# An attention and feed-forward kernel whose planner gets new tables of order rules, with more spare matmuls and more score banks on the full array

## The chip, the core and the metric

The kernel runs on one core of a Trainium2 chip. A core has five engines that run their own instruction streams side by side and meet only at semaphores: TensorE (PE; PEld is its weight load), VectorE (DVE), ScalarE (ACT), GpSimd (POOL) and SyncE (SP), which here issues all DMA transfers. Matmul results land in PSUM, which the program uses as eight banks of 512 float32 columns on 128 partitions. The metric is the time of one execution on the device in microseconds; the median of three runs is 1193.63 us (1188.23 to 1194.63).

## What is computed

```python
xn = _layernorm(x)                                    # x: 1 x 2048 x 512, bfloat16
q, k, v = split_heads(xn @ wqkv)                      # H = 32 heads of 16
scores = einsum("bhqd,bhkd->bhqk", q, k) * 16 ** -0.5
o = einsum("bhqk,bhkd->bhqd", softmax(scores), v)
attn = merge_heads(o) @ wo
ffn = (silu(xn @ w1) * (xn @ w3)) @ w2                # F = 1792
return x + attn + ffn
```

The work that sets the time is the 32 x 2048 x 2048 scores: each is computed twice, goes once through a maximum and once through an exponential.

## The kernel before

**Two passes over the scores.** The 2048 queries are cut into four quarters of 512 and the heads into eight groups of four; a *unit* is 256 queries of one group (128 in the first two units and in the last four groups), 73 units in all. In the first pass (`p1`, line 1319) a matmul puts 128 queries on the partitions of a bank and 512 keys on its columns. One head has 16 numbers, padded to 32 rows, so such a matmul uses a 32-row strip of the array, a quarter of it, and four heads' matmuls can run side by side in four strips. DVE then takes the maximum over two banks in one instruction (line 1364, `part<-ps`, 128 x 1024 numbers), here called a *reduce*. There are 998 of them and 13 of another form (`SPLIT`, lines 1357, 1420, 1423 and 1432), for which ACT prepares half of the work. From the maxima of a unit POOL makes the negated maximum, which goes as two more rows into the padded queries (`Z`, `Zs`, `QT`), by DMA, and in the first and last units by PE (`ident,Z`) and ACT or DVE.

In the second pass (`p2`, line 1601) a matmul puts 128 keys on the partitions and 256 queries on the columns, so that the scores come out transposed and less their maximum; two such matmuls fill a bank, and ACT turns it into exponentials in the tile `PT` (line 1626, or 1657 where two neighbouring banks go through one instruction, a *pair*). The units in pieces of 128 queries take four matmuls for a bank. Instead of a strip, a bank of the second pass can be computed on the full array (*wide*): DMA copies the queries of one head into a matrix `BD` (128 rows, zero outside that head's 32), and a matmul with all 128 rows of keys gives the same scores (`ps<-BD,KT`; line 721, or line 725 where it stands as four column strips among value products). The value products (`ps<-PT,Vaug`, line 725) are four matmuls side by side, one for each head, with 17 columns each: 16 of the value and one of ones, which gives the sum. ACT copies the result to `U`, DMA and POOL make the reciprocal (`Lc`, `Rc`, `R`) and POOL normalises it into `wk_on` or `on_b`; in the last units DVE does this alone.

**The rest** fills PE between scores: the projections (`xnT,w...`), the gate and up products with ACT and POOL making `hT` from them, and the output tiles (`OUT`, `w,hT` 14 matmuls, `wo` and `wol`, with x added by `xr,ident`). The last quarter's output tiles come in two parts, `OUTA` (19 matmuls of 512 columns, parked in `t1`, `a32`, `th` and `zg`) and `OUTB` (2 matmuls, added to the parked part by DVE, line 1147). When a planner's estimate of PE's load is low, a *spare group* is put into a free bank: the identity times `xnT` (`ps<-xnT,ident`), whose result nobody reads. A `p1` matmul may also be issued two or three times over for the same reason.

**What sets the order.** Nothing is looped on the chip: a planner in Python (`_Prog` and the closing loop of `_build`) writes all five streams out. It keeps an estimate of when each engine and each bank is free, asks `pick_dve`, `pick_act`, `pick_pe`, `pick_pool` and `pick_sp` for their earliest next step, and emits the earliest. `pick_pe` (line 2017) chooses among the next `p1` pair, the next second-pass bank, the next group of a tile, a spare group (`fill_cand`) and a wide bank, by limits in `K`. `heat` (line 1961) is its estimate of PE's load over the last 3.413 us; `HEAT_FILL` is the load under which a spare group is put in, `HEAT_WIDE` that under which a bank is taken wide, `HEAT_P1` that under which `p1` is repeated; `A_LEAD` and `ROW_LEAD` say how far ahead of DVE and ACT their matmuls are issued; `PAIR_WAIT`, `PAIR_DEPTH` and `P2_NEAR` bear on pairs. The limits are not the same throughout:

```python
        if p1_n[0] + p2_n[0] >= seg[0] * SEG:
            rule = TUNE[seg[0]] if seg[0] < len(TUNE) else 0
            ...
            for k_, v_ in SETS[rule].items():
                setattr(K, k_, v_)
```

Each time 12 more steps of the two passes have been planned (`SEG`; both passes together have 3072), the defaults `RULES` are set again and the entry of `SETS` that `TUNE` names for this stretch is laid over them.

## Time and profile before

| | us |
|---|---|
| median of three runs | 1193.63 |
| lowest and highest | 1188.23, 1194.63 |
| the profiled execution's own time | 1195.37 |
| its span, first to last instruction | 1193.6 |
| busy: PE, DVE, ACT, POOL | 1120.2, 1167.8, 1167.2, 453.2 |
| mean granted TensorE clock | 0.986 |

The profiled execution is 1.74 us over the median of the runs. A share of busy time counts an instruction from its start to its end, and instructions of one engine overlap at their ends, so an engine that is called busy throughout can still be slower than its shortest pitch; the pitch is read from runs of equal instructions. In rows of groups the columns are: line, engine, operation, tiles, shapes and count; then busy time and mean duration in ns; then idle time of the engine just before them, and what ended most of it. In rows of a timeline the first number is the start and the second the length until the last of the counted instructions ends. The granted clock is 1.00 at full speed.

### The profile page before, as it was taken

How to read it: one execution, taken by the hardware profiler on the slowest of the kernel's cores; microseconds unless marked ns; L12 is line 12 of the kernel's file. 1: busy time of each engine (PE TensorE's matmuls, PEld its weight loads, DVE VectorE, ACT ScalarE, POOL GpSimd, SP SyncE). 2: the span in 40 equal slices, each digit the busy share in tenths (PEclk: the TensorE clock that was granted, in tenths of full speed). 3: DMA queues.
4: the chain of work that ended last, by engine and by line, in shares of the span. 5: the costliest groups of instructions: out<-in, count | busy, mean ns of one | idle time of the engine just before them, and what ended most of it. 6: DMA issues, size and time to landing. Idle time of an engine off the chain costs nothing.

```text
span 1193.6 us, 35219 instructions
## 1 busy us (share of the span) xinstructions
PE 1120.2 (94%) x14470; PEld 517.1 (43%) x14609; DVE 1167.8 (98%) x1090; ACT 1167.2 (98%) x2202; POOL 453.2 (38%) x888
## 2 busy tenths in 40 slices
PE   8999999999999999999999999999999999998998
PEld 4433444443444433344444443433334443455664
DVE  8999999999999999999999999999999999999995
ACT  8899999999999999999999999999999999998998
POOL 7145544244422355324432226533442214541220
PEclk9999999999999999999999999999899999997999
DMA  8232232111111121111111122111110112001000
GB/s 247 76 74 75 70 84 61 38 37 42 33 42 36 35 63 42 34 40 33 41 31 28 34 54 56 42 39 41 30 30 24 35 37 62 23 22 21 19 16 24
DMA packets 141636, 55.88 MB, mean 47 GB/s; under 512 B 103968, under 2 KB 141476, under 8 KB 141476
## 3 DMA queue, kind: packets, MB, share of 16 engines
q1 hardware_dynamic: 141476, 53.63, 17.5%
q8 instruction: 115, 1.88, 0.7%
q14 instruction: 45, 0.37, 0.1%
HBM read 38.93 MB, written 6.74 MB: 38 GB/s over the span
## 4 chain that ended last, share of the span: by engine, by line
ACT 49%; DVE 27%; PE 20%; DMA 2%; issue 2%; POOL 1%; SPq 0%; DVEq 0%; POOLq 0%
ACT PT L1626 35%; DVE part L1364 26%; PE ps L721 7%; ACT PT L1657 7%; PE ps L1601 4%; PE ps L725 4%; PE ps L1319 3%; ACT zg L1037 1%; ACT th L1031 1%; ACT ub L1041 1%; ACT U L1721 1%; ACT RB L1432 1%; ACT kq L909 1%; DMA R<-rd 1%; POOL Rc L1746 1%
## 5 line engine op out<-in xcount | busy, mean ns | idle before, releaser
L1364 DVE TENSOR_REDUCE part<-ps 128x2 f32<-128x1024 f32 x998 | 1134.7, 1212 | 9.6 <-PE ps L1601 5.4
L1626 ACT ACTIVATE PT<-ps 128x512 bf16<-128x512 f32 x1640 | 874.6, 688 | 10.1 <-PE ps L1601 6.3
L1601 PE MATMUL ps<-QT,KT 32*128 32x256 bf16 (+1 forms) x3634 | 475.2, 261 | 15.1 <-ACT PT L1626 3.0
L1319 PE MATMUL ps<-KT,QT 32*128 32x512 bf16 x2158 | 439.8, 387 | 12.7 <-DVE part L1364 5.9
L1601 PEld LDWEIGHTS ps<-QT,KT 32*128 32x128 bf16 x3634 | 169.9, 93 | 179.9 <-ACT PT L1626 72.3
L1657 ACT ACTIVATE PT<-ps 128x1024 bf16<-128x1024 f32 x204 | 222.3, 1116 | 1.5 <-PE ps L1601 1.3
L725 PE MATMUL ps<-PT,Vaug 128*17 128x256 bf16 (+1 forms) x4672 | 193.7, 263 | 3.4 <-DVE part L1364 0.8
L1319 PEld LDWEIGHTS ps<-KT,QT 32*128 32x128 bf16 x2158 | 109.5, 91 | 154.2 <-DVE part L1364 71.2
L721 PE MATMUL ps<-xnT,w 128*128 128x512 bf16 (+3 forms) x583 | 148.0, 320 | 12.3 <-ACT U L1721 4.4
L1746 POOL TENSOR_TENSOR Rc<-Lc,mone 128x8 f32<-128x8 f32 (+1 forms) x69 | 105.0, 1521 | 119.4 <-DMA Lc<-U 118.8
L725 PEld LDWEIGHTS ps<-PT,Vaug 128*17 128x17 bf16 x4672 | 90.7, 90 | 80.7 <-issue 54.1
L721 PE MATMUL ps<-BD,KT 128*128 128x256 bf16 (+1 forms) x676 | 117.5, 268 | 3.7 <-ACT PT L1657 1.8
L1493 POOL TENSOR_TENSOR mx<-part 128x16 f32<-128x16 f32 (+1 forms) x60 | 14.2, 237 | 196.8 <-DVE part L1364 196.8
L721 PE MATMUL ps<-w,hT 128*128 128x128 bf16 (+3 forms) x349 | 81.6, 295 | 3.3 <-ACT U L1721 2.3
L721 PEld LDWEIGHTS ps<-xnT,w 128*128 128x128 bf16 x628 | 47.3, 97 | 83.3 <-issue 41.9
L721 PE MATMUL ps<-xnT,ident 128*128 128x512 bf16 (+3 forms) x244 | 66.5, 329 | 11.0 <-ACT PT L1657 3.8
L1008 POOL TENSOR_SCALAR t<-th 128x512 f32<-128x512 bf16 x56 | 34.9, 623 | 100.5 <-ACT th L1031 98.8
L1012 POOL TENSOR_TENSOR hT<-a,t 128x512 bf16<-128x512 f32 x56 | 71.1, 1269 | 2.7
L721 PEld LDWEIGHTS ps<-BD,KT 128*128 128x128 bf16 x676 | 53.4, 98 | 35.8 <-ACT PT L1626 8.0
L1782 POOL TENSOR_TENSOR on_b<-U,R 128x256 bf16<-128x256 f32 (+1 forms) x33 | 23.4, 710 | 117.4 <-DMA R<-rd 117.1
L1782 POOL TENSOR_TENSOR wk_on<-U,R 128x256 bf16<-128x256 f32 (+1 forms) x36 | 22.9, 637 | 110.2 <-DMA R<-rd 110.2
L1010 POOL TENSOR_TENSOR a<-zg,ub 128x512 f32<-128x512 bf16 x56 | 64.7, 1155 | 0.0
(114 smaller groups left out, 727.4 us busy)
## 6 DMA issues: line engine op xcount, KB each, us to landing
w<-in_B_w_dram SPq DMA_DIRECT2D x112, 128.0 KB
R<-rd SPq DMA_DIRECT2D x55, 128.0 KB
QT<-qd SPq DMA_DIRECT2D x31, 128.0 KB
KT<-kd SPq DMA_DIRECT2D x28, 128.0 KB
BD<-QT SPq DMA_DIRECT2D x220, 10.5 KB
xr<-in_A_x_dram SPq DMA_DIRECT2D x16, 128.0 KB
out_dram<-osb SPq DMA_DIRECT2D x16, 128.0 KB
qd<-kq SPq DMA_DIRECT2D x15, 128.0 KB
```

Of the source, the lines that this page charges most:

```text
L721: return e.matmul(bank(bk)[:, c0 + a:c0 + b], make_lhsT(0, 128), rhs_ap(0)[:, a:b], start=start, stop=stop, **kw)
L725: ins = e.matmul(bank(bk)[32 * i:32 * i + m, c0 + a:c0 + b], make_lhsT(i), rhs if (a, b) == (0, ncols) else rhs[:, a:b], start=start, stop ...
L1008: q.append(_Item(lambda e: e.tensor_scalar(t1[:, :], th[:, ss, :], 1.0, 1.0, ALU.mult, ALU.add), [("th", ss)], [("t1",)], 0.62, 0.72))
L1010: q.append(_Item(lambda e: e.tensor_tensor(a32[:, :], zg[:, ss, :], ub[:, ss, :], ALU.mult), [("zg", ss), ("ub", ss)], [("a32",)], 1.1, 1.25))
L1012: q.append(_Item(lambda e: e.tensor_tensor(hT[:, hslot(idx), :], a32[:, :], t1[:, :], ALU.mult), [("a32",), ("t1",)], [("hT", hslot(idx))] ...
L1319: ins = e.matmul(bank(held[i]), QT[32 * j:32 * j + 32, qs, q * 128:(q + 1) * 128], KT[32 * j:32 * j + 32, g, c_ * 512:(c_ + 1) * 512], sta ...
L1364: redq.append(_Item(lambda e: e.tensor_reduce(dst, banks, AX.X, ALU.max), writes, [("part", par, i_) for i_ in ix[:m]], _c_dve(512 * m), c ...
L1601: ins = e.matmul(bank(b)[:, i * nq:(i + 1) * nq], KT[32 * j:32 * j + 32, g, (k0 + i) * 128:(k0 + i + 1) * 128], QT[32 * j:32 * j + 32, qs, ...
L1626: expq.append(_Item(lambda e: e.activation(PT[:, sl, :], bank(b), ACTF.Exp, scale=SCALE), [("ps", b)], [("PT", sl)], _c_act(512), cb=cb, e ...
L1657: return _Item(lambda e: e.activation(PT[:, s0:s1 + 1:s1 - s0, :], two_banks(b0, b1), ACTF.Exp, scale=SCALE), [("ps", b0), ("ps", b1)], [( ...
L1746: poolq["nrm"].append(_Item(lambda e: e.tensor_tensor(Rc[:, pp, 0:nl], Lc[:, pp, 0:nl], mone[:, 0:nl], ALU.pow), [("Lc", pp), ("mone",)], ...
L1782: poolq["nrm"].append(_Item(lambda e: e.tensor_tensor(onorm[ob][:, oslot(ob, g), q0:q0 + nq], U[:, us, 0:nq], R[:, pp, 0:nq], ALU.mult), [ ...
```

## The change

Two tables of `_build` are replaced, and nothing else. `SETS` grows from 82 to 134 entries and `TUNE` from 254 to 256; before, 38 stretches used the plain defaults, and now 22. `HEAT_FILL` is set in 62 stretches instead of 34.

```diff
     SETS = (
         dict(),
         dict(A_LEAD=0.88, RELAX=0.1),
-        dict(A_LEAD=0.69),
+        dict(PAIR_WAIT=0.15, RELAX=0.05),
+        dict(P2_FRAG=0.0, URG_WAIT=0.05, A_LEAD=0.82, PAIR_WAIT=0.15),
...
     TUNE = (
-        1, 2, 3, 4, 5, 6, 7, 8, 0, 9, 10, 11, 0, 12, 13, 14, 15, 16, 17, 18, 19, 20, 21, 22,
+        1, 2, 3, 4, 5, 6, 7, 8, 9, 10, 11, 0, 12, 13, 0, 14, 15, 16, 17, 18, 19, 20, 21, 22,
...
```

The lines behind the tables stand 52 further down in the new kernel (1319 becomes 1371, 1601 becomes 1653, 721 becomes 773, 725 becomes 777, 1626 becomes 1678, 1657 becomes 1709). In the two orders as a whole, PE's instructions grow from 14611 to 15173. Of the 2048 banks of the second pass, 468 are wide before and 573 now. Spare groups are 311 before and 415 now (345 of them whole matmuls, 70 in four strips). ACT's pairs are 204 before and 160 now. DVE's, POOL's and SP's instructions are the same in kind and number, but for one parked part of an output tile that DVE takes from ACT.

Two places are shown, both on PE. The first is the slots of reduces 941 to 943 (of 1011), in the units of 128 queries near the end. `KT,QT` is the first pass, `QT,KT` the second in strips, `BD,KT` the second on the full array. Before:

```order
L1319 MATMUL ps<-KT,QT 128x512 x2
L1601 MATMUL ps<-QT,KT 128x128 x4
L721 MATMUL ps<-xnT,ident 128x512
L721 MATMUL ps<-xnT,ident 128x384
L1319 MATMUL ps<-KT,QT 128x512 x2
L1601 MATMUL ps<-QT,KT 128x128 x16
L721 MATMUL ps<-xnT,ident 128x512
L1319 MATMUL ps<-KT,QT 128x512 x2
L1601 MATMUL ps<-QT,KT 128x128 x8
```

The same three slots now:

```order
L1371 MATMUL ps<-KT,QT 128x512 x2
L773 MATMUL ps<-BD,KT 128x128 x8
L777 MATMUL ps<-PT,Vaug 17x128 x12
L1371 MATMUL ps<-KT,QT 128x512 x2
L773 MATMUL ps<-BD,KT 128x128 x8
L777 MATMUL ps<-PT,Vaug 17x128 x4
L1371 MATMUL ps<-KT,QT 128x512 x2
L1653 MATMUL ps<-QT,KT 128x128 x4
L773 MATMUL ps<-BD,KT 128x128 x4
L1653 MATMUL ps<-QT,KT 128x128 x4
L773 MATMUL ps<-xnT,ident 128x384
```

Seven banks in strips and three spare groups have become five wide banks, two banks in strips, value products and one spare group.

The second place is the end of PE's stream, from the last but one row of second-pass banks; `w,hT`, `wo` and `wol` belong to output tiles. Before:

```order
L1601 MATMUL ps<-QT,KT 128x128 x12
L721 MATMUL ps<-wol,wk_on 128x512 x3
L725 MATMUL ps<-PT,Vaug 17x128 x4
L1601 MATMUL ps<-QT,KT 128x128 x12
L725 MATMUL ps<-PT,Vaug 17x128 x16
L1601 MATMUL ps<-QT,KT 128x128 x8
L725 MATMUL ps<-PT,Vaug 17x128 x92
L721 MATMUL ps<-wol,wk_on 128x512 x2
L725 MATMUL ps<-PT,Vaug 17x128 x16
L721 MATMUL ps<-wol,wk_on 128x512 x2
```

Now:

```order
L773 MATMUL ps<-w,hT 128x512
L1653 MATMUL ps<-QT,KT 128x128 x12
L773 MATMUL ps<-w,hT 128x512 x3
L1653 MATMUL ps<-QT,KT 128x128 x12
L773 MATMUL ps<-w,hT 128x512 x10
L773 MATMUL ps<-wo,wk_on 128x512 x2
L773 MATMUL ps<-wol,wk_on 128x512 x4
L777 MATMUL ps<-PT,Vaug 17x128 x64
L773 MATMUL ps<-wol,wk_on 128x512 x2
```

The last `OUTA` tile, done in before ahead of these rows, now stands with 14 of its 19 matmuls behind the last score bank, and the last unit's 64 value products stand behind it. Behind the matmuls of the last reduce, 34 second-pass banks follow in before and 37 now; behind the row of the last unit's negated maximum (`ident,Z`), 26 and 30.

193 lines of the change are left out of this document (122 added, 71 removed), and 20 rows, old and new, of the table TUNE.

## The prediction

> **What bounds the kernel now.** I read the page first (busy shares, slices, the chain, the costliest groups), then the stretches of half clock, then the end. Lines of the page:
>
> ```profile
> PE 1120.2 (94%) x14470; PEld 517.1 (43%) x14609; DVE 1167.8 (98%) x1090; ACT 1167.2 (98%) x2202; POOL 453.2 (38%) x888
> ...
> PEclk9999999999999999999999999999899999997999
> ...
> L1364 DVE TENSOR_REDUCE part<-ps 128x2 f32<-128x1024 f32 x998 | 1134.7, 1212 | 9.6 <-PE ps L1601 5.4
> L1626 ACT ACTIVATE PT<-ps 128x512 bf16<-128x512 f32 x1640 | 874.6, 688 | 10.1 <-PE ps L1601 6.3
> L1657 ACT ACTIVATE PT<-ps 128x1024 bf16<-128x1024 f32 x204 | 222.3, 1116 | 1.5 <-PE ps L1601 1.3
> ```
>
> DVE (VectorE) holds 998 reduces, and a run of seven of them shows their pitch: (8.00 - 1.21) / 6 = 1.13 us.
>
> ```profile
> 1164.91 8.00 DVE L1364 TENSOR_REDUCE part<-ps 128x2 f32<-128x1024 f32 x7
> ```
>
> So the question is where DVE does not run at that pitch. Busy time by stretch answers it; columns are length, then busy time of PE, weight load, DVE, ACT and POOL, and the granted clock:
>
> ```profile
> 331.53:338.40 6.87, 6.87 (x109) 3.02 (x107) 6.18 (x6) 6.20 (x14) 0.72 (x1) 0.75 0.09 26
> 614.84:621.70 6.86, 5.98 (x62) 2.30 (x64) 6.14 (x6) 6.28 (x11) 5.06 (x6) 0.75 0.09 29
> 846.94:857.20 10.26, 9.79 (x61) 2.83 (x63) 8.05 (x9) 7.83 (x15) 1.60 (x5) 0.67 0.21 50
> 1089.29:1109.80 20.51, 19.08 (x352) 11.83 (x344) 16.48 (x16) 16.65 (x31) 4.70 (x9) 0.58 0.10 21
> sum 44.50, PE 41.72 PEld 19.99 DVE 36.84 ACT 36.96 POOL 12.09; mean PE 10.43 PEld 5.00 DVE 9.21 ACT 9.24 POOL 3.02
> ```
>
> ```profile
> 0.00:13.96 13.96, 10.99 (x93) 7.87 (x93) 10.48 (x29) 9.66 (x23) 6.55 (x25) 1.00 0.89 287
> 13.96:331.53 317.57, 299.62 (x3496) 129.56 (x3536) 316.57 (x283) 310.53 (x576) 140.43 (x251) 1.00 0.26 67
> 338.40:614.84 276.44, 261.05 (x3088) 115.31 (x3117) 276.42 (x250) 276.30 (x533) 108.49 (x212) 1.00 0.16 40
> 621.70:846.94 225.24, 213.28 (x2559) 94.42 (x2576) 224.82 (x204) 223.91 (x416) 90.65 (x172) 1.00 0.16 41
> 857.20:1089.29 232.09, 217.44 (x3084) 102.82 (x3105) 232.00 (x211) 231.94 (x444) 81.56 (x181) 1.00 0.13 32
> 1109.80:1172.90 63.10, 60.16 (x1257) 38.23 (x1258) 62.47 (x61) 62.51 (x132) 13.39 (x29) 1.00 0.08 17
> 1172.90:1193.60 20.70, 15.92 (x355) 8.94 (x357) 8.21 (x26) 15.38 (x21) 0.00 (x0) 0.95 0.08 27
> ```
>
> The span is 13.96 us before the first reduce, 1158.94 us of reduces, and 20.70 us behind the last. Between, DVE stands 44.50 - 36.84 = 7.66 us in the four stretches that begin at half clock, and only 1.00 + 0.02 + 0.42 + 0.09 + 0.63 = 2.16 us in all the rest. A stop also loses the 1.21 - 1.13 = 0.08 us by which reduces overlap; some 20 reduces follow a stop there, so the half clock costs about 7.66 + 1.6 = 9.3 us.
>
> The half clock itself lasts 3.41, 3.41, 6.83 and 17.07 us, multiples of 3.41:
>
> ```profile
> 331.53:334.94 3.41, 3.41 (x35) 1.23 (x33) 3.25 (x3) 3.10 (x7) 0.72 (x1) 0.50 0.03 8
> 614.84:618.25 3.41, 3.08 (x18) 1.12 (x16) 2.69 (x3) 3.05 (x5) 1.69 (x2) 0.50 0.14 45
> 846.94:853.77 6.83, 6.36 (x32) 1.61 (x33) 4.87 (x6) 4.76 (x9) 1.60 (x5) 0.50 0.29 70
> 1085.88:1089.29 3.41, 2.55 (x55) 1.50 (x50) 3.41 (x4) 3.41 (x6) 0.28 (x2) 1.00 0.10 24
> 1089.29:1106.36 17.07, 15.80 (x291) 9.91 (x286) 13.17 (x13) 13.24 (x25) 3.31 (x6) 0.50 0.12 23
> ```
>
> What stands ahead of the longest, in the 3.41 us from 1085.88, by shape, and a row that gives the time of a column:
>
> ```profile
> L1601 PE MATMUL ps<-QT,KT 32*128 32x128 bf16 x32 | 1.8, 217 | 0.2 <-ACT PT L1657 0.2
> L1319 PE MATMUL ps<-KT,QT 32*128 32x512 bf16 x6 | 1.2, 384 | 0.6 <-ACT PT L1626 0.4 <-DVE part L1364 0.2
> L725 PE MATMUL ps<-PT,Vaug 128*17 128x128 bf16 x16 | 0.5, 240 | 0.1
> L721 PE MATMUL ps<-xnT,ident 128*128 128x512 bf16 x1 | 0.4, 389 | 0.0
> ```
>
> ```profile
> 1178.39 1.04 PE L721 MATMUL ps<-w,hT 128*128 128x512 bf16 x4
> ```
>
> I call load the columns streamed, each counted with the quarter of the array that it fills (score matmuls and value products a quarter, others whole). Here (32 x 128 + 6 x 512 + 16 x 128) / 4 + 512 = 2816 columns. By the x4 row a column takes (1.04 - 0.39) / 3 / 512 = 0.42 ns, so 3.41 us hold 8060 columns: load 0.35. Counted in this way over the order of before, in windows of three reduces (3 x 1.13 us), the mean is 0.58, and 40 of 997 windows lie under 0.40. All four stops follow at once on one of these 40 (those from reduce 277, 527, 730 and 941). Of the 40, which stand in 29 places, four were followed by half clock.
>
> **The change, part by part.** Only the two tables differ, so no kind of instruction is added; the counts are from the two orders.
>
> Head, reduces, GpSimd, DMA: 0. DVE's rows are the same up to the last reduce (998, with the same 13 split rows), PE's the same for the first 57 rows; POOL and SP hold 892 and 1044 instructions in both. Steps move against them: the copies that fill BD stand earlier or later on SP's queue. Their cover is the unit's lead before its banks; uncovered, it would show as reduces or exponentials that wait for a bank, which is part of the 2.16 us. I leave that at 2.16, between 0 and 5.
>
> Thin load: windows under 0.40 go from 40 to 15, the mean from 0.58 to 0.60. At one stop for each ten, 1.5 stops are left. A short stop costs 6.87 - 6.18 us and two lost overlaps of 0.08, 0.85 us, and the mean of the four is 9.3 / 4 = 2.3. I take the short one, as the stretch around reduce 941, whose long half clock fed itself on 128-column work, rises to 0.56. So 1.3 us remain of 9.3 (bounds 0 and 3.5): -8.0 us.
> The Trainium skill (TensorE: Matmul & The Clock Gate, Terms) prices a throttled time at its length times the missing share, an estimate of 30.72 x 0.5 = 15.4 us here instead of 9.3; with the same 1.5 stops, the sum would fall to 1195.4 - 15.4 + 2.6 + 3.9 = 1186.5 us. The trace does not bear it out: DVE stands 7.66 us in and behind these stretches, since work stands ahead of it in the banks.
>
> More load to carry: 105 score banks move from quarter matmuls (1580 to 1475) to full-array matmuls over BD (468 to 573), and spare groups stream 140,500 columns for 118,700. A bank is two matmuls of 256 columns: on the full array 2 x 0.11 us of PE to itself, as quarters four banks in 0.22, 0.05 each; 105 x 0.16 = 17 us, and 21,900 x 0.42 ns = 9 us. These 26 us lie in PE's 1193.6 - 1120.2 = 73.4 us of idle time, and each reduce's two matmuls still stand ahead of them in its slot. I take 0 (bounds 0 and 26).
>
> Fewer pairs: 160 exponentials of two banks for 204. ACT's rows near the end show both prices:
>
> ```profile
> 1174.55 0.64 ACT L1626 ACTIVATE PT<-ps 128x512 bf16<-128x512 f32 x1
> 1175.03 1.08 ACT L1657 ACTIVATE PT<-ps 128x1024 bf16<-128x1024 f32 x1
> 1175.94 0.67 ACT L1626 ACTIVATE PT<-ps 128x512 bf16<-128x512 f32 x1
> ...
> 1187.42 0.87 ACT L1626 ACTIVATE PT<-ps 128x512 bf16<-128x512 f32 x1
> ```
>
> A bank alone takes 0.48 us to the next start and a pair 0.91, so 44 x 0.05 = 2.2 us more on ACT. What hides it is ACT's lead in the middle, where DVE stops only for 2.16 us; without that cover it adds up to 2.2.
>
> The end is the loss. Rows of PE in before:
>
> ```profile
> 1185.72 0.69 PE L1601 MATMUL ps<-QT,KT 32*128 32x128 bf16 x8
> 1186.34 1.46 PE L725 MATMUL ps<-PT,Vaug 128*17 128x128 bf16 x92
> ...
> 1188.33 0.40 PE L725 MATMUL ps<-PT,Vaug 128*17 128x128 bf16 x16
> ```
>
> ACT runs without a gap to 1188.29, three banks in 0.48 + 0.91 = 1.39 us. Behind the negated maximum of the last unit (ident,Z) before has 26 banks to go, after 30: 4 x 0.46 = +1.8 us; behind the last reduce's matmuls it is 34 and 37, +1.4. I take 1.6. Then PE's last score bank ends at 1186.41, 1.9 us before ACT does; the 92 value products run in that time, and the last 16 follow the last exponential. In the new order 16 matmuls of 512 columns (14 of the last quarter's sum, two of another) stand there first, 16 x 0.217 = 3.5 us, and then all 64 value products, 64 / 92 x 1.46 = 1.0 us: they end 4.7 us after the last score bank, where those of before end at 1188.73, 2.3 us after it. +2.4 us, less a little since three banks, not two, are issued last: 2.3. So +3.9 (bounds: +0.8 if ACT was less behind and PE's rest ran in its waits, +5).
>
> Sum, against the profiled execution's own 1195.37 us: -8.0 + 0 + 0 + 3.9 = 1191.3 us. That execution stood 1.74 us over the median of the three shown, 1193.63; their spread (1188.23 to 1194.63) is what a different number of stops would make.
>
> **The rivals.**
> The end is hidden (0.24): ACT arrives with fewer banks behind it and PE's late matmuls fit in its waits. For it: PE is busy 15.92 of the last 20.70 us. Against: PE works in order, and the 16 stand ahead. Time 1187.4 with 1.3 us of stops, 1186.1 with none: faster.
> A stop costs half its length (0.03): the four of before then cost 30.72 / 2 = 15.4 us and 1.5 of them 2.6, which gives 1186.5; DVE's 7.66 us speak against it.
> The stops stay (0.11): thin load isn't what sets them, or new ones grow where the new order is thin (reduces 139, 170, 184). Then 1195.4 + 3.9 = 1199.3, or slower with one long stop more. Speaking for it: 36 of 40 thin windows went unpunished.
> By the Trainium skill (TensorE: Matmul & The Clock Gate, What's actually happening) the clock falls after an idle window of some 3.4 us, and PE wasn't idle in any: by that rule this rival would be the case. The trace speaks against it: 2.55 us of 3.41 busy, then half clock.
> PE becomes the bound (0.10, slower): the 26 us of added matmul time push reduces' matmuls back. It decides from 8.3 us of the 26 on the path: 1191.3 + 8.3 = 1199.6; at half of them, 1204. Against it: 2.16 us of DVE idle at full clock.
>
> **How the numbers follow.** My forecast has 0.52, and its own range is 1188 to 1195. What a measurement can tell here is about 0.5% of 1193.63, 6.0 us: faster is under 1187.7, slower over 1199.6. The hidden end and the half price are faster, 0.27, with 0.02 of mine at its edge; of the stops that stay half is slower, with PE as the bound 0.15; the same has 0.56. The range, 1185 to 1199, takes in the hidden end and half of the stops that stay, and leaves out PE as the bound and the worst stops.
>
> **What would show it.** Granted clock over 0.99 with at most two short stops (a mean of 0.986 again means the stops stayed). DVE idle between first and last reduce under 5 us, and the last reduce ending near 1165. Behind it 24 to 25 us, with ACT's last exponential some 17 us after the last reduce, and the value products behind the 16 long matmuls. I am wrong if DVE waits for score banks at full clock, or if the end is as long as before.

## The result, and the profile after

Over 20 executions of each, the changed kernel takes 1196.97 us (1192.32 to 1204.50) and the kernel before 1192.44 us (1188.17 to 1201.79): a ratio of 1.0040, 95% interval 1.0021 to 1.0059. The change makes the kernel slower by 0.4%; two more comparisons of the two kernels, in the table below, give 1.0012 and 1.0036, with intervals that reach down to 0.9987 and 1.0000. The prediction of 1191.3 us had the sign wrong; its range of 1185 to 1199 us holds the time.

The profiled execution of the changed kernel is a low one of its 20: 1193.87 us, with a span of 1192.1 us. The page, where L1416 is the reduce, L1678 the single exponential and L1709 the pair:

```profile
PE 1123.6 (94%) x15037; PEld 529.2 (44%) x15171; DVE 1166.7 (98%) x1091; ACT 1166.2 (98%) x2245; POOL 452.0 (38%) x888
...
PEclk9999999999999999999999999999999999999999
...
L1416 DVE TENSOR_REDUCE part<-ps 128x2 f32<-128x1024 f32 x998 | 1133.2, 1216 | 6.9 <-PE ps L1653 3.5
L1678 ACT ACTIVATE PT<-ps 128x512 bf16<-128x512 f32 x1728 | 918.8, 715 | 6.5 <-PE ps L1653 2.4
L1709 ACT ACTIVATE PT<-ps 128x1024 bf16<-128x1024 f32 x160 | 177.0, 1123 | 0.3 <-PE ps L1653 0.2
```

Busy time by stretch, cut at the first reduce, at the one stretch of half clock and at the last reduce:

```profile
0.00:14.25 14.25, 10.84 (x93) 7.77 (x93) 10.47 (x29) 9.67 (x23) 6.99 (x25) 1.00 0.91 285
14.25:1095.69 1081.44, 1025.24 (x13132) 467.69 (x13250) 1077.20 (x969) 1069.37 (x2057) 428.77 (x831) 1.00 0.18 46
1095.69:1099.11 3.42, 3.08 (x29) 1.66 (x30) 1.50 (x2) 2.17 (x5) 0.00 (x0) 0.50 0.05 7
1099.11:1168.36 69.25, 65.91 (x1418) 42.30 (x1427) 68.57 (x67) 68.54 (x141) 15.76 (x32) 1.00 0.09 18
1168.36:1192.10 23.74, 18.52 (x369) 9.79 (x371) 8.93 (x26) 16.45 (x24) 0.46 (x1) 0.98 0.07 24
```

Three things are read from these. Of the 30.72 us of half clock between the reduces, 3.42 us are left. The end takes 23.74 us instead of 20.70. And DVE, which stood 2.16 us at full clock before, now stands 1081.44 - 1077.20 = 4.24 us ahead of the half clock and 69.25 - 68.57 = 0.68 us behind it; with 3.42 - 1.50 = 1.92 us at half clock it is idle for 6.84 us. Counted by starts of neighbouring reduces against their pitch of 1.13 us, the changed kernel loses 7.9 us between first and last reduce, and 5.6 of them at four places: 1.13 us at 79 and 83, 1.62 at 122, 2.06 at 1094 and 0.76 at 1142 us. (By the same count the profile of before loses 11.8 us, most of it in and just behind its half clock. The count leaves out a wait that begins behind another instruction of DVE, here 0.87 us at 1083 us, where PE waits 1.06 us for a copy into `BD`.) What PE waits for there, in the chain of waits (total, times, longest):

```profile
PE ps L773 <- POOL Z L1522: 2.7, 2, 2.0
PE ps L777 <- DMA BD<-QT: 2.6, 2, 1.5
...
PE ps L1653 <- DMA QT<-Zs: 1.1, 1, 1.1
```

The longest, row by row:

```profile
1093.74 0.45 POOL L1834 TENSOR_TENSOR wk_on<-U,R 128x128 bf16<-128x128 f32 x1 [6.01 <-DMA R<-rd]
1094.15 1.01 POOL L1798 TENSOR_TENSOR Rc<-Lc,mone 128x4 f32<-128x4 f32 x1
1095.14 0.21 POOL L1520 TENSOR_SCALAR Z<-negm 128x4 bf16<-128x4 f32 x1
...
1095.70 0.29 PE L773 MATMUL ps<-ident,Z 128*128 128x128 bf16 x1 [1.96 <-POOL Z L1522]
...
1097.10 1.22 DVE L1416 TENSOR_REDUCE part<-ps 128x2 f32<-128x1024 f32 x1 [1.97 <-PE ps L1653]
```

POOL works in order. The negated maximum is there at 1092.9 us (DVE's row 1092.70, 0.17 long), but `Z` stands behind a product that waits for the DMA of `R`. PE stands 1.96 us, DVE as long, and 0.01 us before PE starts again the clock falls to half; of the 3.41 us ahead of that, PE was busy for 1.36.

**The measure used below.** Single executions differ by some 10 us, and most of that follows the mean granted clock: from it, (1 - clock) x 2 x time is the time at half clock, and over the 29 to 35 executions of the kernel before in each of the five groups of runs, the time rises by 0.34, 0.35, 0.35, 0.35 and 0.34 us for each us at half clock, which accounts for 86 to 89% of its variance. (A group was run on one chip, the kernel before beside the others; the groups are those of the five sections below.) So each kernel gets two numbers: its median time at half clock, and its *clear time*, the mean of time less 0.34 us per us at half clock. The clear time has a standard error of 0.3 to 0.7 us. In the five groups the kernel before has clear times of 1185.7, 1185.4, 1185.7, 1185.7 and 1186.1 us, at 26 to 34 us of half clock, so kernels of different groups are compared by it. The slope is that of the kernel before; the 44 executions of the changed kernel give 0.39, with a standard error of 0.04. By that slope the gap of 7.3 us between the two kernels would be 6.6, and the 4.1 us that the mended queue brings below would be 3.7.

| kernel | median us | ratio to before, 95% | half clock us | clear us |
|---|---|---|---|---|
| before (five groups) | 1193.86 to 1196.24 | 1 | 26.3 to 33.5 | 1185.7 |
| changed, first 20 | 1196.97 | 1.0040 (1.0021 to 1.0059) | 13.2 | 1193.0 |
| again_before | 1191.45 | 0.9964 (0.9934 to 0.9993) | 17.9 | 1185.2 |
| again_after | 1199.14 | 1.0012 (0.9987 to 1.0037) | 18.0 | 1193.7 |
| after_other_end | 1203.19 | 1.0039 (1.0012 to 1.0065) | 27.7 | 1192.6 |
| after_no_spare_load | 1249.22 | 1.0406 (1.0360 to 1.0451) | 229.4 | |
| changed_third | 1199.89 | 1.0036 (1.0000 to 1.0072) | 20.4 | 1192.9 |
| no_three_waits | 1205.03 | 1.0069 (1.0033 to 1.0104) | 25.3 | 1196.3 |
| value_products_first | 1202.96 | 1.0042 (1.0007 to 1.0077) | 21.7 | 1195.6 |
| both_mended | 1204.93 | 1.0069 (1.0035 to 1.0103) | 26.5 | 1196.8 |
| z_moved_right | 1198.28 | 1.0024 (0.9997 to 1.0051) | 13.2 | 1193.1 |
| z_and_strips | 1195.94 | 1.0019 (0.9996 to 1.0042) | 13.2 | 1192.0 |
| before_with_other_end | 1198.67 | 1.0049 (1.0022 to 1.0077) | 31.2 | 1188.3 |
| shifted_code | 1197.22 | 1.0021 (0.9992 to 1.0050) | 12.0 | 1192.5 |
| sp_queue_mended | 1191.18 | 0.9979 (0.9958 to 1.0000) | 4.8 | 1188.9 |
| before_lc_late | 1197.18 | 1.0026 (1.0007 to 1.0045) | 29.9 | 1186.8 |
| before_more_load | 1198.16 | 1.0025 (0.9999 to 1.0052) | 15.6 | 1192.0 |
| sp_one_place | 1202.24 | 1.0043 (1.0013 to 1.0073) | 22.9 | 1194.5 |
| sp_queue_again | 1190.94 | 0.9971 (0.9945 to 0.9997) | 6.0 | 1188.9 |
| sp_queue_and_end | 1192.35 | 0.9965 (0.9938 to 0.9991) | 7.2 | 1189.0 |

`again_before` is the kernel before itself, and its 12 executions still differ by 0.36% from the 29 of its own group, which hold twice the half clock: 0.4% in one comparison of medians can be the clock alone. The clear time is what tells these kernels apart. `after_no_spare_load` has none, since its half clock lies far outside the range from which the slope was taken.

### The profile page after: what moved, and what is told of

It is laid out like the page before. It is cut to its first block, busy times and chain, and to the rows that moved or that the text cites. A ratio compares the mean times of both kernels' runs of the same rounds, so it can differ in the third digit from the quotient of the medians.

```text
span 1192.1 us, 36419 instructions
## 1 busy us (share of the span) xinstructions
PE 1123.6 (94%) x15037; PEld 529.2 (44%) x15171; DVE 1166.7 (98%) x1091; ACT 1166.2 (98%) x2245; POOL 452.0 (38%) x888
## 4 chain that ended last, share of the span: by engine, by line
ACT 67%; DVE 14%; PE 12%; DMA 3%; issue 2%; SPq 1%; POOL 1%
ACT PT L1678 51%; DVE part L1416 14%; ACT PT L1709 8%; PE ps L773 5%; PE ps L777 3%; PE ps L1371 2%; PE ps L1653 2%; ACT zg L1089 2%; ACT th L1083 1%; ACT ub L1093 1%; ACT U L1773 1%; DMA rd<-Rc 1%; ACT RB L1484 1%; DMA R<-rd 1%; ACT kq L961 1%
## 5 line engine op out<-in xcount | busy, mean ns | idle before, releaser
L1416 DVE TENSOR_REDUCE part<-ps 128x2 f32<-128x1024 f32 x998 | 1133.2, 1216 | 6.9 <-PE ps L1653 3.5
L1678 ACT ACTIVATE PT<-ps 128x512 bf16<-128x512 f32 x1728 | 918.8, 715 | 6.5 <-PE ps L1653 2.4
L1653 PE MATMUL ps<-QT,KT 32*128 32x256 bf16 (+1 forms) x3420 | 457.0, 258 | 8.8 <-DMA QT<-Zs 1.1
L1371 PE MATMUL ps<-KT,QT 32*128 32x512 bf16 x2158 | 431.5, 384 | 8.3 <-DVE part L1416 4.2
L1653 PEld LDWEIGHTS ps<-QT,KT 32*128 32x128 bf16 x3420 | 161.5, 93 | 167.1 <-ACT PT L1678 70.2
L1709 ACT ACTIVATE PT<-ps 128x1024 bf16<-128x1024 f32 x160 | 177.0, 1123 | 0.3 <-PE ps L1653 0.2
L773 PE MATMUL ps<-xnT,w 128*128 128x512 bf16 (+3 forms) x612 | 153.3, 309 | 12.4 <-ACT PT L1678 3.4
L773 PE MATMUL ps<-BD,KT 128*128 128x256 bf16 (+1 forms) x790 | 135.1, 265 | 3.1 <-ACT PT L1709 0.9
L773 PE MATMUL ps<-xnT,ident 128*128 128x512 bf16 (+3 forms) x314 | 80.5, 323 | 10.0 <-DVE part L1416 3.1
L777 PE MATMUL ps<-BD,KT 128*32 128x256 bf16 (+1 forms) x1848 | 83.5, 265 | 2.9 <-DMA BD<-QT 2.6
L1834 POOL TENSOR_TENSOR wk_on<-U,R 128x256 bf16<-128x256 f32 (+1 forms) x36 | 22.9, 635 | 139.6 <-DMA R<-rd 139.6
L773 PEld LDWEIGHTS ps<-BD,KT 128*128 128x128 bf16 x790 | 60.9, 98 | 32.5 <-ACT PT L1678 7.2
```

The costliest lines, as they stand in the source:

```text
L773: return e.matmul(bank(bk)[:, c0 + a:c0 + b], make_lhsT(0, 128), rhs_ap(0)[:, a:b], start=start, stop=stop, **kw)
L777: ins = e.matmul(bank(bk)[32 * i:32 * i + m, c0 + a:c0 + b], make_lhsT(i), rhs if (a, b) == (0, ncols) else rhs[:, a:b], start=start, stop ...
L1371: ins = e.matmul(bank(held[i]), QT[32 * j:32 * j + 32, qs, q * 128:(q + 1) * 128], KT[32 * j:32 * j + 32, g, c_ * 512:(c_ + 1) * 512], sta ...
L1416: redq.append(_Item(lambda e: e.tensor_reduce(dst, banks, AX.X, ALU.max), writes, [("part", par, i_) for i_ in ix[:m]], _c_dve(512 * m), c ...
L1653: ins = e.matmul(bank(b)[:, i * nq:(i + 1) * nq], KT[32 * j:32 * j + 32, g, (k0 + i) * 128:(k0 + i + 1) * 128], QT[32 * j:32 * j + 32, qs, ...
L1678: expq.append(_Item(lambda e: e.activation(PT[:, sl, :], bank(b), ACTF.Exp, scale=SCALE), [("ps", b)], [("PT", sl)], _c_act(512), cb=cb, e ...
```

## The experiments

### The two kernels again, the other end, and no spare load

The first two are the kernels unchanged. The third takes the tables of before from entry 238 on:

```diff
     TUNE = (
...
-        99, 118, 75, 45, 119, 118, 120, 0, 121, 12, 41, 20, 122, 89, 109, 123, 0, 20, 124, 12, 125, 76, 126, 19,
-        29, 69, 76, 38, 127, 21, 128, 85, 73, 109, 129, 130, 131, 132, 0, 133,
+        99, 118, 75, 45, 119, 118, 120, 0, 121, 12, 41, 20, 122, 89, 109, 123, 0, 20, 124, 12, 125, 76, 49, 21,
+        38, 46, 87, 72, 12, 28, 0, 0, 0, 126, 127, 108, 58, 126,
```

The fourth keeps the changed order and lets each spare group stream 16 columns, which leaves out spare work only and nothing of the output:

```diff
-                P.pe(col_groups(bk, lambda i, z=32: ident[:, 32 * i:32 * i + z], lambda i: xnT[:, 0, 0:128 * k], 128 * k,
-                                own=P.pe_mode == "col" and not P.pe_full),
+                own = P.pe_mode == "col" and not P.pe_full
+                P.pe(col_groups(bk, lambda i, z=32: ident[:, 32 * i:32 * i + z], lambda i: xnT[:, 0, 0:16], 16, own=own),
```

> The kernel before, unchanged, to see the granted clock of many of its executions, which the first result gives for the changed kernel alone. Theory A (the change did take half-clock time away, and its order has a longer floor, that is a longer time without any half clock): the mean granted clock here is lower than the changed kernel's 0.994, about 0.988 to 0.990 (25 to 30 us at half clock), with a median near 1192.5 us, so that the floor lies at 1183 to 1186. Theory B (the stops are as frequent in both, and only the end is longer): the clock is 0.993 to 0.995 here too, and the floor 1188 or more.

> The changed kernel, unchanged, on the same chip as the others of this call. Both theories: median 1196 to 1198 us, mean clock 0.992 to 0.996. A second profile tells whether PE's waits at full clock that the first one shows (for copies into BD near 122 us, for the last rows of the queries near 80 us, for POOL's negated maximum near 1094 and 1142 us) stand in the order or came once: in theory A at least three of the four come again, 3 us or more together.

> The changed kernel up to entry 238 of its table of rules, then the old table's entries: the last output tile's 16 matmuls no longer stand between the last score bank and the last value products. If that piece is what the end costs (the prediction's 2.3 us), the time behind the last reduce falls from 23.7 to about 21.4 us and the median by 2 to 3 us, to about 1194.5. If the end's length is set by the banks that ACT still has to do (37 here as in the changed kernel), it stays at 23 to 24 us and the median within 1 us of the changed kernel's.

> The changed kernel with each spare group cut to 16 columns, all else in the same order with the same waits. If thin load sets the half clock, the time at half clock rises from some 13 us to over 60 us (mean clock under 0.97) and the time to 1210 us or more, about 0.34 us for each us more. If the half clock comes from stalls of PE alone, or spare groups don't reach it, the clock stays over 0.99 and the time at 1194 to 1198.

The changed kernel has less half clock (13 to 20 us against 26 to 34) and a clear time longer by 7.3 us, as theory A has it. Its losses at full clock come back at the same places: in three profiles of it 1.13, 1.47 and 0.83 us at 79 and 83 us, 1.62, 1.32 and 2.13 at 122, 2.06, 1.62 and 1.72 at 1094, and 0.76, 1.24 and 1.28 at 1143. `again_before` loses nothing at the first of these places and no more than 0.8 us near 1090, at half clock. The wait near 80 us is not the changed order's alone: the first profile of before loses 1.00 us at 82.19 us and that of `before_more_load`, with before's order, 0.89, both where PE waits for `QT<-Zs`. In all three profiles of the changed kernel half clock begins at or within 3 us behind the wait at 1094 us: at 1095.69, 1098.39 and 1097.70.

Without spare load the clock bears out the cause that the prediction gave to it. The page of `after_no_spare_load`:

```profile
PEclk9999899879799998879979999977867999976899
...
L1416 DVE TENSOR_REDUCE part<-ps 128x2 f32<-128x1024 f32 x998 | 1140.8, 1215 | 48.0 <-PE ps L1653 28.5
```

With the order kept and only columns taken away, half clock goes from 18.0 us (`again_after`, of the same group) to 229.4, in stretches over the whole span, and the time rises by 50 us. That is 0.24 us for each us, less than the 0.34 expected. `after_other_end` tells little: its order near the end thinned out (10.24 us of half clock from 1169.46 us), and its clear time stayed. The planner gives another order for each table, so a table is not a clean edit; apart from `before_with_other_end`, the later edits change single instructions in a finished order.

### Three waits and the end, moved by hand

A pass behind the planner takes operations out of an engine's list, puts them ahead of another, and numbers the semaphore counts anew (engine, first, last, ahead of). In `no_three_waits`:

```diff
         P.check()
+        P.rearrange(MOVES)
...
+    MOVES = (('pool', 849, 850, 847), ('pool', 871, 872, 869))
```

Two wide banks near 122 us (`STRIPS` holds their numbers, 130 and 132) are issued as strips there too, at the same places in PE's order:

```diff
-                    P.pe(fw, reads, writes, "col", None, kpb * _c_mm(nq), name="w2_%d" % n, first="act")
+                    if n in STRIPS:
...
+                        op = P.pe(f, reads + qh_keys(qs, q0, nq, (j,)) + qt_keys(qs, q0, nq, "QTr0")
+                                  + qt_keys(qs, q0, nq, "QTr1"), writes, "col", None, kpb * _c_mm(nq),
+                                  name="w2_%d" % n, first="act")
...
+                    else:
+                        P.pe(fw, reads, writes, "col", None, kpb * _c_mm(nq), name="w2_%d" % n, first="act")
```

In `value_products_first` the value products of the last bank go ahead of the long matmuls:

```diff
+    MOVES = (('pe', 6178, 6193, 6172),)
```

`both_mended` has all of these.

> The changed kernel as it is, as the measure for the three others of this group. Over the 32 timed executions of it so far, the time follows 1192 to 1193 us plus 0.34 to 0.45 us for each us that TensorE's clock stood at half (from the mean granted clock). Both theories: median 1196 to 1199, with the same waits at full clock near 80, 122, 1094 and 1143 us that two profiles showed.

> The changed kernel with the order of every engine kept, but for two things: the two full-array score banks that stand first behind the BD copies near 122 us are computed as quarter matmuls (they need no copy), and on GpSimd the two Z instructions stand ahead of the normalisation's multiply and reciprocal (which wait for a DMA) at the places near 1094 and 1143 us. Theory A (the changed order is longer by its own waits at full clock): DVE's loss at these three places, 1.62 + 2.06 + 0.76 = 4.4 us in one profile and 1.32 + 1.62 + 1.24 = 4.2 us in the other, falls under 1 us, and the time at a given share of half clock falls by 3 to 4 us, to 1189 plus its stops. Theory B (the waits are slack: ACT, whose share of the chain rose from 49% to 67%, sets the pace, so that a wait taken away is given back by the next one): the loss turns up elsewhere and the time at a given share stays within 1 us of the changed kernel's.

> The changed kernel with one block of TensorE's order moved: the last 64 value products stand ahead of the last six output-projection matmuls (wo, wol), behind the last quarter's nine hT matmuls. Theory A (the end is longer because the value products stand behind the long matmuls): they start when ACT's last exponential is done, about 1.3 us sooner, and the stretch behind the last reduce falls from 23.7 to 22.2 us. Theory B (the end is set by the sum of TensorE's work behind the last reduce): the six matmuls now stand in front of the last output instead, and the stretch stays at 23.4 us or more.

> The two edits before together. Theory A: both gains add, 1187.5 us plus the stops, a median of 1191 to 1193 us, 5 us under the changed kernel and level with or under the kernel before. Theory B: within 2 us of the changed kernel.

All three edits made the kernel slower. Two reasons are plain. The `Z` pairs that were moved were the ones next behind those that wait, so the normalisation was put off by a step where nothing waited for it, and the waits stayed (2.81 us of PE at 1098 us in `no_three_waits`). The strips did what they should for their own two banks: near 122 us `no_three_waits` loses 0.13 and 0.55 us in place of 2.13. In `both_mended` and `z_and_strips`, which have the same strips, PE waits there for the copies into `BD` of the next wide banks, and DVE still loses 1.01 and 1.59 us.

The other is the end. In `value_products_first`:

```profile
1195.65 1.31 ACT L1743 ACTIVATE PT<-ps 128x1024 bf16<-128x1024 f32 x1
...
1196.98 1.07 PE L811 MATMUL ps<-PT,Vaug 128*17 128x128 bf16 x64
...
1199.06 0.69 DVE L1217 TENSOR_SCALAR zg<-ps 128x512 f32<-128x512 f32 x1 [5.62 <-PE ps L807]
1199.67 0.68 DVE L1233 TENSOR_TENSOR osb<-ps,th 128x512 bf16<-128x512 f32 x1
1200.27 0.30 DVE L1791 STREAM_TRANSPOSE U<-ps 128x128 f32<-128x128 f32 x1
```

The value products start as ACT ends, as wanted, and are done at 1198.05 us; but DVE also works in order, and takes the last unit only behind two instructions that now come later: 2.2 us lost, an end of 24.5 us. The rest of this kernel's 2.7 us of clear time over `changed_third` may lie at 122, 1100 and 1151 us, places that were not touched: there its one profile loses 2.88, 2.06 and 2.64 us against 2.13, 1.72 and 1.28. At the last of them a DMA landed later: near 1143 us the row of `Lc<-U` starts 1.92 and 1.94 us ahead of `Rc` in two profiles of the changed kernel, and 3.09 us in this one. Why it landed later was not settled.

### The right pairs, the end put into the kernel before, and shifted code

In `z_moved_right` the pairs that wait are the ones moved:

```diff
+    MOVES = (('pool', 845, 846, 843), ('pool', 867, 868, 865))
```

`z_and_strips` has the two strips as well. `before_with_other_end` is the kernel before with the changed tables from entry 242 on. `shifted_code`:

```diff
+                    def g(e, more=24 if n_fill[0] == 0 else 0):
+                        for i in range(more):
+                            e.matmul(bank(bk)[:, 0:32], ones_t[:, :], ones_t[:, 0:32], start=True, stop=True)
```

> The changed kernel with two pairs of Z instructions moved on GpSimd: those that ran at 1095.14 and 1142.68 us in its profile now stand ahead of the normalisation's multiply and reciprocal (1093.74 and 1138.63 us), nothing else. In the group before, the pairs next behind these had been moved by mistake, which left the waits where they were. Theory A (the changed order is longer by its own waits at full clock): the waits for Z (2.0 to 2.1 us near 1094, 0.8 to 1.3 us near 1143) go, the time at a given share of half clock falls from 1193 to 1190.5, and the half clock that follows the first of them at once becomes rare. Theory B (each wait taken away is given back elsewhere): within 1 us of 1193.

> The same, and the two full-array banks that stand behind the BD copies near 122 us as quarter matmuls. Theory A: also the 1.3 to 2.1 us of loss near 122 us go, 1189 at the same share. Theory B: within 1 us of 1193.

> The kernel before with the changed kernel's settings from entry 242 of its table on: 33 score banks are left behind the last reduce's matmuls, and 14 hT matmuls and four of the output projection stand behind the last score bank, as in the changed kernel. Theory A: the stretch behind the last reduce grows from 20.5 to 23 us and the time at a given share of half clock from 1185.5 to 1188. Theory B (the end is hidden): 20.5 us and 1185.5.

> The changed kernel with 24 more small matmuls (32 columns) on TensorE in the head, where it waits for data, so that all its later instructions lie 48 places further in its code; the order of all the rest is the same. Theory L (a rival that the last group raised: the kernels edited at the end or at two places waited 1 to 2 us longer at places that were not edited, where a DMA landed 1.2 us later; it is the place of the code's own fetches that decides): the time at a given share of half clock moves by 1.5 us or more from 1193, and the waits near 122, 1094 and 1143 us change. Theory A: 1193 within 0.7, and the same waits.

Here theory A fell in part: with `Z` out of the way the clear time stayed at 1193.1 us, and with the strips it came to 1192.0. The wait near 1094 us had only changed hands. In `z_and_strips`, where `Z` was done at 1094.1 us:

```profile
1096.11 0.28 ACT L1818 ACTIVATE U<-ps 128x128 f32<-128x128 f32 x1 [2.03 <-POOL wk_on L1879]
```

ACT copies a unit's value product into a buffer of `U` from which an earlier unit's product `wk_on` must first have been made; `wk_on` is late because `R` is. PE's next matmul needed the bank that ACT was to empty. That points past `Z` and ACT to the normalisation, which comes too late.

The end is shown by the reverse: in `before_with_other_end` it grows from 20.53 us (`again_before`) to 22.48, and the clear time by 2.6 us, to 1188.3. `shifted_code` leaves the clear time at 1192.5, so where the code lies does not explain the 7 us. Its single waits did change, against theory A: in its profile DVE loses 0.41 us near 1097 us in place of 1.6 to 2.1, and no half clock follows there. The size of one wait in one profile is therefore not what the place costs in a mean execution.

The end of `again_before`, busy time by stretch:

```profile
1168.57:1189.10 20.53, 16.39 (x357) 8.94 (x353) 8.20 (x25) 15.23 (x21) 0.00 (x0) 0.98 0.08 27
```

And of `before_with_other_end`:

```profile
1174.82:1197.30 22.48, 18.81 (x310) 9.40 (x306) 7.89 (x22) 14.69 (x24) 0.46 (x1) 1.00 0.08 26
```

### SP's queue

Why is the normalisation late? SP's rows in `again_before`, near 1080 us:

```profile
1079.79 0.57 SPq L1755 DMA_DIRECT2D R<-rd  x1
1080.40 0.54 SPq L1742 DMA_DIRECT2D Lc<-U  x1
...
1082.28 3.14 SPq L1450 DMA_DIRECT2D BD<-QT  x4
1085.48 1.12 SPq L1512 DMA_DIRECT2D QT<-Zs  x2
1086.64 0.44 SPq L1751 DMA_DIRECT2D rd<-Rc  x1
...
1088.50 0.60 SPq L1755 DMA_DIRECT2D R<-rd  x1
```

And in the changed kernel:

```profile
1080.01 3.14 SPq L1502 DMA_DIRECT2D BD<-QT  x4
1083.21 1.11 SPq L1564 DMA_DIRECT2D QT<-Zs  x2
1084.37 0.57 SPq L1794 DMA_DIRECT2D Lc<-U  x1
...
1085.56 2.99 SPq L1502 DMA_DIRECT2D BD<-QT  x4
1088.60 0.44 SPq L1803 DMA_DIRECT2D rd<-Rc  x1
...
1091.03 0.60 SPq L1807 DMA_DIRECT2D R<-rd  x1
```

`Lc<-U`, the first step of the normalisation, now stands behind the four copies into `BD` and starts 4.0 us later; `rd` and `R` follow it behind four more copies. The product `wk_on` comes at 1093.74 us, where `again_before` has it at 1092.20, with its `U` at 1094.13.

`sp_queue_mended` puts this right at four places of SP's order, and moves one instruction of POOL (engine, which, ahead of). The first three moves are `Lc`, `rd` and `R` near 1080 us; then follow `Lc` near 1140, a copy into `BD` ahead of a weight near 121, and `QT<-Zs` and `Z` near 73 us:

```diff
+    MOVES = (('sp', 971, 965), ('sp', 977, 972), ('sp', 979, 974), ('sp', 1025, 1022), ('sp', 126, 125), ('sp', 124, 129), ('sp', 73, 71), ('sp', 74, 71), ('pool', 65, 64))
```

`before_lc_late` brings the changed kernel's order into the kernel before, at the one place near 1080 us:

```diff
+    MOVES = (('sp', 964, 972), ('sp', 972, 979), ('sp', 980, 979), ('sp', 975, 979))
```

`before_more_load` keeps the order of before and issues 61 groups twice, in the stretches in which its half clock began:

```diff
+                P.pe(twice(f) if n in RED_2 else f, reads, writes, "row", rows, again * _c_mm(512) * deep, name="p1_%d" % n, first="dve")
...
+                    P.pe(twice(fw) if n in WIDE_2 else fw, reads, writes, "col", None, kpb * _c_mm(nq), name="w2_%d" % n, first="act")
...
+                ff = col_groups(bk, lambda i, z=32: ident[:, 32 * i:32 * i + z], lambda i: xnT[:, 0, 0:128 * k], 128 * k,
+                                own=P.pe_mode == "col" and not P.pe_full)
+                P.pe(twice(ff) if n_fill[0] in FILL_2 else ff,
```

> The changed kernel with SP's queue put in another order at four places, all else kept: near 1080 us the copy Lc<-U (1084.37) goes ahead of the four BD copies and two QT<-Zs that it stood behind, and rd<-Rc and R<-rd (1088.60, 1091.03) ahead of the next BD copies; near 1140 us Lc<-U goes ahead of three BD copies; near 121 us the BD copy that the first full-array bank needs goes ahead of a weight load and another copy; near 73 us QT<-Zs goes ahead of rd<-Rc and R<-rd, and on GpSimd the second Z instruction ahead of a product that waits for a DMA. Theory S (SP's order makes the normalisation late, and wk_on, ScalarE's U and the Z matmul wait for it): wk_on near 1093.7 us comes 2 to 3 us sooner, the waits near 80, 122, 1094 and 1143 us (5 us together) fall under 1.5, and the time at a given share of half clock falls from 1193 to 1189 or 1190. Theory B (such waits are given back): within 1 us of 1193.

> The kernel before with SP's order changed at one place, near 1080 us, to what it is in the changed kernel: Lc<-U behind four BD copies and two QT<-Zs, rd<-Rc and R<-rd behind four more BD copies. Theory S: wk_on, at 1092.2 us before, comes 1.5 to 3 us later, ScalarE's U or the Z matmul waits for it, DVE loses 0.5 to 2 us near 1095 us, and the time at a given share of half clock rises from 1185.6 to 1186 to 1187.5. Theory B: 1185.6 within 0.4, no wait at that place.

> The kernel before, its order kept, with 61 of its matmul groups issued twice (34 spare groups, 19 full-array score banks and 8 reduces' matmuls, some 12 us of TensorE in all), only in the thin stretches near 330, 610, 840, 1045, 1080 and 1102 us, where its half clock began in several profiles. Theory A (thin load sets the half clock, and adding load is free): the half clock falls from some 26 to 33 us to under 15, the time at a given share stays at 1185.6 within 1, and the median comes to 1190 or 1191, under both kernels. Rival P (TensorE's time is not free there): the half clock falls, but reduces' matmuls come late, and the time at a given share rises by 2 us or more. Rival R (half clock is not set by load at these places): it stays over 25 us.

The mended queue takes the clear time from 1193 to 1188.9 us and the half clock to 4.8 us; theory S gave 1189 or 1190. Its page:

```profile
PEclk9999999999999999999999999999999999999999
...
L1449 DVE TENSOR_REDUCE part<-ps 128x2 f32<-128x1024 f32 x998 | 1132.4, 1215 | 1.0 <-PE ps L1686 0.8
```

Its stretch of reduces and its end, busy time by stretch:

```profile
13.91:1161.38 1147.47, 1115.23 (x14707) 511.13 (x14707) 1146.48 (x1037) 1139.46 (x2202) 445.70 (x863) 1.00 0.18 45
1161.38:1185.10 23.72, 19.46 (x373) 9.78 (x371) 8.92 (x27) 16.45 (x24) 0.46 (x1) 0.97 0.08 24
```

DVE's loss against its pitch is 2.24 us in all, none of it at 79, 83, 122 or 1143 us, and between first and last reduce there is no half clock in this execution, one of the two fastest of its 12. The product `wk_on` starts at 1085.46 us, 10.0 us behind the first of the four copies into `BD` (1075.43); in the changed kernel it was 1093.74 - 1080.01 = 13.7 us. In `before_lc_late` the same wait appears where there was none; ACT's row, with its `U` ready to be copied, and the reduce behind it:

```profile
1099.43 0.28 ACT L1754 ACTIVATE U<-ps 128x128 f32<-128x128 f32 x1 [4.50 <-POOL wk_on L1815]
...
1100.44 1.23 DVE L1397 TENSOR_REDUCE part<-ps 128x2 f32<-128x1024 f32 x1 [3.93 <-PE ps L1352]
```

PE waits 4.4 us for it, and DVE 3.93 us at this reduce and 1.11 at the next, more than the 0.5 to 2 us expected; half clock begins within the wait, at 1097.94 us. The clear time rises by only 1.1 us (standard error 0.7), as expected, so this execution shows the wait longer than its mean cost.

`before_more_load` goes to rival P: half clock falls to 15.6 us, but the clear time rises by 6.3. By its page DVE waits for more than in the two profiles of the kernel before, whose same rows end in 9.6 and 6.0 us; 8.1 us of its waits fall at full clock, against 3.2 and 1.7 there:

```profile
L1376 DVE TENSOR_REDUCE part<-ps 128x2 f32<-128x1024 f32 x998 | 1135.8, 1215 | 12.7 <-PE ps L1613 7.2
```

### One place of the queue, the mended queue again, and the end

`sp_one_place` has the first three moves of `sp_queue_mended` alone. `sp_queue_and_end` has all, and in `MOVES` also PE's operations 6178 to 6193 ahead of 6172 (the last 64 value products) and DVE's 1072 to 1075 ahead of 1071, and:

```diff
-                if to_dve():
+                if to_dve() and tg != NT - 1:
```

> The changed kernel with SP's order mended only near 1080 us (Lc<-U ahead of BD copies and QT<-Zs, rd<-Rc and R<-rd ahead of the next BD copies). Theory S: the wait near 1094 us (1.6 to 2.1 us of DVE) goes, with most of the half clock that followed it; those near 80, 122 and 1143 us stay. The time at a given share of half clock falls from 1193 to 1191, the half clock from 13 to 20 us to about 10.

> The changed kernel with SP's queue mended at all four places, once more: 1189 us plus 0.34 us for each us at half clock, of which there are about 5; a median of 1190 to 1192 and under the kernel before of the same group by 1 to 4 us. If the gain was the luck of one chip: 1193 or more at the same share.

> The same and another end: the last 64 value products ahead of the last quarter's output projections on TensorE, the last unit's four VectorE instructions ahead of the sum of the output tile before, and the last partial sum copied out by ScalarE, which has nothing left to do, in place of VectorE. By the rows of the mended kernel's end, the value products end 1.3 us sooner, VectorE takes the last unit's normalisation at once, and the last output sum starts 1.0 us sooner: the stretch behind the last reduce falls from 23.7 to 22.7 us, the time at a given share from 1189 to 1188. If another engine takes the wait over: 23.7 as before.

The gain repeats: 1190.94 us and a clear time of 1188.9 again, 0.9971 (0.9945 to 0.9997) of the kernel before. One place alone gives nothing: its wait is gone, but that near 1145 us grows from 1.2 to 3.0 us, and the clear time is 1194.5. The normalisations of these last units follow one another; that a step won at one place is spent at the next is read from this one profile.

The move near 1080 us has a price of its own. `Lc<-U` now holds SP for 0.66 us ahead of the four copies into `BD`, and in the profiles of `sp_one_place`, `sp_queue_again` and `sp_queue_and_end` PE waits 1.61, 1.90 and 1.76 us for such a copy. In `sp_queue_again`:

```profile
1080.25 0.41 PE L810 MATMUL ps<-BD,KT 128*32 128x128 bf16 x16 [1.90 <-DMA BD<-QT]
...
1081.19 1.22 DVE L1449 TENSOR_REDUCE part<-ps 128x2 f32<-128x1024 f32 x1 [1.72 <-PE ps L1404]
```

In all three a stretch of 10.24 us at half clock begins within 3 us behind this wait, between 1081 and 1086 us, where the changed kernel had none. The changed kernel's first profile waits 1.06 us there, its second and that of `sp_queue_mended` not at all; why was not settled.

The end of `sp_queue_and_end` is 22.65 us long in its profile, 1.1 us shorter than 23.72, as expected; in the timed executions this does not show (clear time 1189.0, with a standard error of 0.6). Against the kernel before, the three runs of the mended queue give 0.9979, 0.9971 and 0.9965. The kernel before gave 0.9964 against itself (`again_before`), so these medians alone do not show a gain over it: the clear time is still 3 us longer, and the half clock, 4.8 to 7.2 us against 26, makes up for that. The changed kernel was not run in these groups; by the ratios to the kernel before, the mended ones take 0.3 to 0.8% less than it.

## Why the prediction was wrong

**The failed step is "Head, reduces, GpSimd, DMA: 0".** It named the place ("the copies that fill BD stand earlier or later on SP's queue. Their cover is the unit's lead") and took the cover as given: "I leave that at 2.16, between 0 and 5". The order was there to be read: near 1080 us it shows `Lc<-U` ahead of the copies before and behind them after. With SP's queue mended, one POOL instruction moved with it and all else kept, the clear time falls by 4.1 us, in two groups of runs, which is what this step cost. The reverse in the kernel before, at one place, costs 1.1 us with a standard error of 0.7. That this order is the cause is shown for the four places and the POOL instruction together; how they share the 4.1 us is not, since they are not independent, and one place alone gave nothing.

**Thin load, -8.0 us: the mechanism held, the size did not.** Load sets the half clock here: the same order with spare groups cut has 229 us of it, and the order before with more load 15.6 instead of 26.3. But the sum took away the stops of one execution of before, with 30.72 us of half clock, as if none were added, and the count of thin windows came from an order in which nobody waits. In all three profiles of the changed kernel half clock begins at or just behind the wait at 1094 us, and in two of the three mended ones within 3 us behind the new wait near 1081; that a wait makes the load thin and so brings the half clock is argued from these places, not shown by an edit of its own. At 0.34 us each, the 13 to 20 us that the changed kernel has cost 4.5 to 7 us, where 1.3 us were taken; the 26 to 33 us of the kernel before cost 9 to 11. In the two groups that hold both kernels the gain is 5.3 and 2.8 us in place of 8. With the queue mended, 4.8 to 7.2 us of half clock remain, and the step would have been nearly right.

**The price of half clock** was right: 9.3 us for 30.72, 0.30 us for each, against a slope of 0.34 to 0.35 over 157 executions. The Trainium skill (TensorE: Matmul & The Clock Gate, Terms) gives a penalty of the throttled time times the missing share, 0.5 here; the measurement gives less; that work standing ahead in the banks is the reason was only argued. The skill also has the clock fall after an idle window of some 3.4 us (same page, What's actually happening); `after_no_spare_load` had PE busy 96% of its span and 229 us of half clock, so it is not idleness alone, and the measurement decides.

**More load, 0 of 26 us:** held for this order. In `sp_queue_mended`, which has all of it, DVE loses 2.24 us in all, and 4.8 in `sp_queue_again`, most of that at half clock, besides its wait for `BD` near 1081 us. It isn't free in general: 12 us of doubled matmuls at other places cost 6.3 us of clear time.

**Fewer pairs, 0:** held, by the same row. **The end, +3.9:** +3.0 in the profile; in the reverse +2.6 in clear time and +1.95 in the profile. The rows:

```profile
1182.22 0.42 PE L1653 MATMUL ps<-QT,KT 32*128 32x128 bf16 x12
...
1182.57 2.33 PE L773 MATMUL ps<-w,hT 128*128 128x512 bf16 x9
...
1183.50 1.31 ACT L1709 ACTIVATE PT<-ps 128x1024 bf16<-128x1024 f32 x1
...
1186.13 1.07 PE L777 MATMUL ps<-PT,Vaug 128*17 128x128 bf16 x64
```

The value products end 1187.20 - 1182.64 = 4.6 us after the last score bank (4.7 predicted, though the two terms given for it, 3.5 and 1.0, add up to 4.5), behind the long matmuls as said. ACT's last exponential ends 1184.81 - 1168.36 = 16.5 us behind the last reduce, 1.1 us more than before, not 1.6.

**The sum.** 1185.7 us of clear time before, +3.0 for the end, +4.1 for SP's queue, gives 1192.8; measured 1193.0. Since the 4.1 is itself the 1193.0 less the mended 1188.9, this says no more than that the 3.2 us left in the mended kernel are about its end. The half clock saved takes 3 to 5 us of these 7 back. The prediction took -8.0 and +3.9, together -4.1 where the medians moved by +4.5: the queue's 4.1 us and the 3 to 5 us of half clock that were not saved make up most of the difference, and neither alone would have turned the sign clearly. Of its rivals, none had this mechanism: the end was not hidden, PE did not become the bound, and the stops stayed in part. What it named as proof against it came: DVE waits for score banks at full clock (idle for 6.84 us between first and last reduce, 4.92 of them at full clock, where under 5 in all was predicted), and the last reduce ends at 1168.36 us, not near 1165. Its base was also a poor one: the profiled 1195.37 us stood 2.9 us over the median of 20 executions.

## What to carry to other kernels

Where one engine issues all transfers, its queue is a resource like any other: when an order changes, read for each long chain (here `Lc`, `Rc`, `rd`, `R`, `wk_on`) what now stands ahead of its first transfer, and count the issue time of that, before its cover is taken as given. A move that brings one copy forward puts off those behind it: look there for the next wait. A wait that is mended where it shows may only change hands; follow it back until something is late that waits for nothing else, and mend every place of the chain at once: here one place gave nothing and four gave 4.1 us. When single executions differ by more than the effect, take the cause of the spread out by a regression on what each execution records (here the granted clock) before comparing medians.

## What the runs showed of the hardware that was not expected

Half clock came in stretches of 3.41 us and its multiples with PE busy: `after_no_spare_load` has 24 such stretches between the reduces, while no single wait of PE in its chain of waits is longer than 1.6 us there. Their sum differs from execution to execution of one kernel by a factor of more than four (12 to 55 us in the first group of the kernel before), and with it the time by 17 us.

Four copies into `BD` hold SP for 3.14 us, while one of them lands 1.82 us (median of 276) after its row starts. The Trainium skill (DMA: Bandwidth & Descriptors, Issuing engines are not separate DMA queues) calls the issue time usually small against the transfer; for these copies of 5 to 10 KB it is 0.79 us of 1.82, and here it decides.

A small transfer does not always land in the same time: `Lc<-U` has a median of 1.87 us and a longest of 3.64 in the changed kernel. Of the 125 copies `Lc`, `rd` and `BD` there with a packet of the instruction queue in the 2.9 us behind their start, 8 took over 2.9 us, of the 289 others 5. That code loading is the cause is not shown by this.
